# Placing a projection's copy and remainder between the casts of a linear-attention and FFN kernel

## The chip, the cores and the metric

The kernel runs on one core of a Trainium2 chip. The metric is the device time of one execution in microseconds. The kernel before took 695.48 us, the median of three runs (694.21 to 696.63).

## What is computed

A linear attention over 8 batches, 8 heads, 576 positions and 32 memory slots is followed by a feed-forward block with a SiLU over the 4608 rows that the attention gives.

```python
def _attn_ref(q, k, v, phi):
    a = np.exp(phi - np.max(phi, axis=2, keepdims=True))
    a = a / (np.sum(a, axis=2, keepdims=True) + 1e-09)
    k_m = np.einsum('bhsm,bhsd->bhmd', a, k)
    v_m = np.einsum('bhsm,bhsd->bhmd', a, v)
    scores = 1.0 / np.sqrt(q.shape[-1]) * np.matmul(q, k_m.transpose(0, 1, 3, 2))
    scores = scores - np.max(scores, axis=-1, keepdims=True)
    attn = np.exp(scores)
    attn = attn / (np.sum(attn, axis=-1, keepdims=True) + 1e-09)
    return np.matmul(attn, v_m)

def _moe_ref(x, w_in, w_out):          # x: (4608, 512), d_ff = 2048
    h = x @ w_in
    return (h * (1.0 / (1.0 + np.exp(-h)))) @ w_out
```

## The kernel before

The value product and the first FFN matrix are joined: instead of forming the attention's output and then multiplying it with w_in, the kernel multiplies v_m with w_in, once per batch and head. This product is P. It comes in four blocks of 512 columns per batch (`p_mm`, matmuls at line 657 into the PSUM tile `bg`). Every number that a large matmul uses is split in two: a rounded high part, made on ScalarE, and the remainder, made on VectorE. For P these are the copy at line 682 and the subtraction at line 684 (`p_split`), both into the tile `pm`, one after the other. Three matmul terms (hi by hi, hi by lo, lo by hi) take the place of one exact product.

The FFN then runs in slots. A slot makes h for two blocks of 128 columns (`ffn1s`, line 852: twelve matmuls, of which the fifth and sixth are the first that read P's remainder), activates it (line 868 or 870, ScalarE, into `gbuf`), and makes seven sums of the quarters of the result, the forms of a Strassen-like scheme (`forms`). In a slot's forms, ScalarE casts three high parts (line 873) and, once VectorE has made the sums (874, 877, 878), four more (883); VectorE makes the remainders of the first three (884) and of the last four (885). In two slots of a batch, where ScalarE has an exponential to do, VectorE does all of it (880, 881). The forms are multiplied with w_out in the next slot (`st_step`, line 894, 21 matmuls into four PSUM banks named `sum`). So TensorE's order in slot s is: h of slot s, then what else is due (P, the products of phi with k and v, the scores), then the output products of slot s - 1.

The first two batches (b = 0 and 1) use a plain scheme (`ffn1`, lines 704 and 746). Batches b = 2 to 7 have 16 slots each. A table of events (`ev`, `run`) says in which slot the attention of the next batch does its steps: phi's maximum is subtracted in slot 1 (slot 3 for b = 2; lines 322 and 325), the exponential (329) and the first half of the phi-kv product (`e_mm`, 348) come in slots 2 and 3 (4 and 5 for b = 2), the second half in slot 5 (7 for b = 2). `e_mm` ends with the normalisation: two sums (366), two reciprocals (368) and the scaled copies `kvn` (372 on ScalarE, 374 on VectorE). One of its two results lies in the fourth `sum` bank, so the last output products of the slot wait until `kvn` has been read out. The scores of the next batch are computed in slot 7 (`s_all`), transposed on VectorE out of PSUM: two short pieces of 64 columns (404), of which one lies in the fourth `sum` bank too, and two long ones (406).

P's third and fourth blocks are made in the batch that uses them: the third in slot 3 (slot 2 for b = 2, slot 0 for b = 7) and the fourth in slot 5 (slot 2 for b = 7); h reads them from slot 4 and from slot 6 on. `run` issues P's matmuls, copy and remainder ahead of a slot's other events but behind the slot's forms, and holds VectorE's other events behind both (`last_split`, `last_p`, through `behind`, an order without a semaphore). TensorE and ScalarE follow the program's order; on VectorE the scheduler orders what `behind` leaves free.

```python
        todo.sort(key=lambda e: e[0] not in (p_mm, p_pair))
        last_p.clear()
        for fn, a in todo:
            ...
                    for other in [last_split[-1]] + last_p:
                        behind(i, other)
```

Of the kernel before, what the change touches and what calls it, by code (L numbers as in the profile page):

```python
# [16 lines left out]
ALU = mybir.AluOpType  # L17
# [3 lines left out]
B, S, H, M, D = 8, 576, 8, 32, 64  # L21
# [6 lines left out]
JW = 512  # L28
# [8 lines left out]
FULLC = S // P  # L37
# [13 lines left out]
def attn_ffn_kernel(  # L51
# [9 lines left out]
    nc = tc.nc  # L61
# [326 lines left out]
    def s_all(b):  # L388

        sc = at[b]["sc"] = sb.tile([P, 2, S], F32, tag="x" if b == 2 else "y", name=f"sc{b}", bufs=1)  # L390
        bg = bgtile()
        left = [spare_bank()[:, :LEFT], accs()[3][:, Q + KVW : Q + KVW + LEFT]] if b > 3 else beside_h(LEFT)
        kvT = at[b]["kvT"]
        for hf, f, n in ((0, 0, CUT), (1, 0, CUT), (1, CUT, LEFT)):
            for r in range(NR):
                for p in range(2):
                    to = left[p] if f else bg[:, p, hf * CUT : hf * CUT + n]
                    nc.tensor.matmul(
                        to[M * r : M * (r + 1)],
                        kvT[D * p : D * (p + 1), 0, r],  # L400
                        at[b]["q", hf][D * p : D * (p + 1), r, f : f + n],
                        start=not f or b < 4 or p == 0, stop=True, skip_group_check=True,
                    )
        short = [nc.vector.transpose(sc[:, p, 512:], left[p]) for p in range(2)]
        for p in range(2):
            i = nc.vector.transpose(sc[:, p, :512], bg[:, p])
            for other in (*short, last_split[-1]):
                behind(i.ins, other)
# [449 lines left out]
    def exp_slots(b):  # L858
        return () if b == B - 1 else (4, 11) if b == 2 else (2, 11)

    def forms(b, t, j, h):


        g = form_src
        h = live["h"]
        o = b % 2 * LEFT
        if t == 0:
            nc.scalar.activation(gbuf[:, :MAIN], h[0], AF.Silu)  # L868
        for i in range(2 * t):
            nc.scalar.activation(gbuf[:, i * CUT : (i + 1) * CUT], h[i][:, :CUT], AF.Silu)  # L870
            nc.scalar.activation(gleft[:, 2 * j + i, o : o + LEFT], h[i][:, CUT:WIDE], AF.Silu)  # L871
        hi, lo = form_high[j % 2], form_low[j % 2]
        nc.scalar.activation(hi[:, :3], g[:, 1:4], AF.Copy)  # L873
        nc.vector.tensor_tensor(  # L874
            g[:, 4:6], g[:, :1].broadcast_to([P, 2, P]), g[:, 1:3], op=ALU.subtract
        )
        nc.vector.tensor_tensor(g[:, 6], g[:, 1], g[:, 5], op=ALU.subtract)  # L877
        s4 = nc.vector.tensor_tensor(g[:, 7], g[:, 3], g[:, 6], op=ALU.subtract)  # L878
        if t * NP + j in exp_slots(b):
            nc.vector.tensor_copy(hi[:, 3:], g[:, 4:])  # L880
            last_split.append(nc.vector.tensor_tensor(lo, g[:, 1:], hi, op=ALU.subtract))
            return hi, lo
        nc.scalar.activation(hi[:, 3:], g[:, 4:], AF.Copy)  # L883
        behind(nc.vector.tensor_tensor(lo[:, :3], g[:, 1:4], hi[:, :3], op=ALU.subtract).ins, s4)
        last_split.append(nc.vector.tensor_tensor(lo[:, 3:], g[:, 4:], hi[:, 3:], op=ALU.subtract))  # L885
        return hi, lo

    def product(bank, place, part, k, w, first):
# [110 lines left out]
    def ev(b, slot, fn, *a):  # L999
        events.setdefault((b, slot), []).append((fn, a))  # L1000
# [43 lines left out]
    for b in range(B):  # L1044
        n = b + 1
        if b == 0:
            for j in range(2, DFF // CW):
                ev(b, 2 * j - 1.5, p_mm, b, j * CW, CW)
        elif b == 1:
            ev(b, 0, win_save)  # L1050
            for j in range(1, NJ):
                ev(b, 4 * j - 3, p_mm, b, j * JW, JW)
            for j in range(NP):
                ev(b, 1.5 * j + 2, w_forms, j, 0)
                ev(b, 1.5 * j + 2.5, w_forms, j, 1)
        else:
            ev(b, 0, win_load, b, 3)
            ev(b, 0 if n == B else 3 if b > 2 else 2, p_mm, b, 2 * JW, JW)
            if b > 2:
                ev(b, 3, s_norm, b, SECOND)  # L1060
                ev(b, 4, s_back, b, SECOND)
                ev(b, 4, s_low, b, SECOND)
            ev(b, 2 if n == B else 5, p_mm, b, 3 * JW, JW)
            if n < B:
                steady(b, n)
            continue
        at_slot = (
            (4, 5, 6, 7.5, 9, 9.5, 11.5, 12.5, 13, 13.5, 13.5, 14) if b == 0
            else (1, 2, 3, 5, 9, 10, 10, 11, 12, 13, 13, 14)
        )  # L1070
        mx, sub, ex, em, tr, s0, s1, sx, se, ss, sn, sk = at_slot
        ev(b, mx, phi_max, n)
        if n == 1:
            ev(b, sub, phi_allmax, n, (0, 1), (0,))
            ev(b, sub + 0.5, phi_allmax, n, (0, 1), (1,))
        else:
            for i in range(3):
                ev(b, sub, phi_fold, n, i)
        ev(b, sub + 0.5, phi_sub, n)
        ev(b, ex, phi_exp, n)  # L1080
        ev(b, em, e_mm, n)
        ev(b, 14 if b == 0 else em + 1, load_kv, n + 1, range(FULLC if b == 0 else 2))
        ev(b, tr, e_tr, n)
        ev(b, em, load_q, n, 1)
        if n == 1:
            ev(b, s0, s_mm, n, 0)
            ev(b, s1, s_mm, n, 1)
        else:
            ev(b, s0, s_all, n)
        ev(b, s1, load_q, n + 1, 0)  # L1090
        ev(b, sx, s_max, n, ALL)
        ev(b, sx, s_sub, n, ALL)
        ev(b, se, s_exp, n, ALL)
        ev(b, ss, s_sum, n, ALL)
        ev(b, sn, s_norm, n, ALL)
        ev(b, sk, s_back, n, ALL)
        ev(b, sk, s_low, n, ALL)
        ev(b, sk, load_phi, n + 1)
        if b == 0:
            ev(b, 14, p_mm, n, 0, JW)  # L1100
        else:
            for k in range(3):
                ev(b, 12 if k == 2 else 6 + k, win_load, n, k)
            for k in range(2):
                ev(b, 12 + 2 * k, p_mm, n, k * JW, JW)
# [124 lines left out]
    def finish(tiles):  # L1230
# [10 lines left out]
        elif prev[0] == "st" and tiles[0] == 0:  # L1241
            st_step(*prev[1:])

    def run(b, slot):
        todo = events.pop((b, slot), [])
        todo.sort(key=lambda e: e[0] not in (p_mm, p_pair))
        last_p.clear()
        for fn, a in todo:
            n = len(nc.cur_bb.bb.instructions)
            fn(*a)  # L1250
            for i in list(nc.cur_bb.bb.instructions)[n:]:
                if i.engine == DVE and fn not in (p_mm, p_pair, s_all, *((e_mm,) if b > 2 else ())):
                    for other in [last_split[-1]] + last_p:
                        behind(i, other)

    for b in range(B):
        if b == 1:
            whole.close()
            ctx.enter_context(in_order(ACT))
        for s in range(NFC if b > 1 else 0):  # L1260
            t, j = divmod(s, NP)
            h = ffn1s(b, t, j)
            part = forms(b, t, j, h)
            run(b, s)
            finish(range(NI))
            prev = ("st", b, t, j, part)
        for fc in range(NFC if b < 2 else 0):
            if b == 0 and fc < 2:
                for part in range(2):
                    for fn, a in events.pop((b, fc + part / 2), []):  # L1270
                        fn(*a)
                continue
            h = ffn1(b, fc)
            gs = split(silu(b, fc, h))
            for part in range(2):
                if b == 0:
                    finish((2 * part, 2 * part + 1))
                traced = nc.cur_bb.bb.instructions
                n = len(traced)
                for fn, a in events.pop((b, fc + part / 2), []):  # L1280
                    fn(*a)
                if b == 0:
                    for i in list(nc.cur_bb.bb.instructions)[n:]:
                        if i.engine == ACT:
                            behind(i, last_silu[-1])
                        elif i.engine == DVE and fc > 10:
                            behind(i, last_split[-1])
            if b:
                finish(range(NI))
            prev = ("main", b, fc, gs)  # L1290
        if b % 2:
            for n in range(NLS):
                gs = left_split(b, n)
                if b > 1:
                    run(b, NFC + n)
                finish((0, 1, 2, 3))
                prev = ("left", b, n, gs)
# [52 lines left out]
```

## Time and profile before

| What | Value |
|---|---|
| median of three runs | 695.48 us (694.21 to 696.63) |
| profiled execution | 695.39 us |
| its span, first to last instruction | 693.6 us |
| TensorE matmul, busy | 674.0 us (97%), 5932 instructions |
| TensorE weight load, busy | 598.7 us (86%) |
| VectorE, busy | 517.6 us (75%), 1088 instructions |
| ScalarE, busy | 382.1 us (55%), 758 instructions |
| mean granted TensorE clock | 0.998 of full speed |
| DMA | 93.92 MB, 135 GB/s mean |

A matmul's end is modelled, and matmuls overlap, so TensorE's 97% is not all progress: pauses show in the starts of the matmuls. Times in the rows further down count from the span's start. Each row gives the start, the duration, the engine (PE is TensorE, PEld its weight loads, DVE VectorE, ACT ScalarE), the line of the kernel, the operation and its tiles, and in brackets the idle time of the engine before it with what ended that.

### The profile page before, as it was taken

How to read it: one execution, taken by the hardware profiler on the slowest of the kernel's cores; microseconds unless marked ns; L12 is line 12 of the kernel's file. 1: busy time of each engine (PE TensorE's matmuls, PEld its weight loads, DVE VectorE, ACT ScalarE, POOL GpSimd, SP SyncE). 2: the span in 40 equal slices, each digit the busy share in tenths (PEclk: the TensorE clock that was granted, in tenths of full speed). 3: DMA queues.
4: the chain of work that ended last, by engine and by line, in shares of the span. 5: the costliest groups of instructions: out<-in, count | busy, mean ns of one | idle time of the engine just before them, and what ended most of it. 6: DMA issues, size and time to landing. Idle time of an engine off the chain costs nothing.

```text
span 693.6 us, 14807 instructions
## 1 busy us (share of the span) xinstructions
PE 674.0 (97%) x5932; PEld 598.7 (86%) x5932; DVE 517.6 (75%) x1088; ACT 382.1 (55%) x758; POOL 0.7 (0%) x6
## 2 busy tenths in 40 slices
PE   8899999999999899989999899999999999999997
PEld 3578777888888899979999799988999879889997
DVE  4997899788847488778775688776876767777653
ACT  3879784544535455744645446564654546655551
POOL 0000000000000000000000000000000000000000
PEclk9999999999999999999999999999999999999999
DMA  9998965314451361344320434125431204210001
GB/s 340 356 347 256 347 254 218 109 45 160 146 162 44 130 220 62 111 156 150 132 92 20 166 132 156 69 85 181 152 123 37 72 2 140 79 72 17 32 1 45
DMA packets 38228, 93.92 MB, mean 135 GB/s; under 512 B 4752, under 2 KB 22032, under 8 KB 34576
## 3 DMA queue, kind: packets, MB, share of 16 engines
q1 hardware_dynamic: 37136, 90.22, 37.7%
q10 hardware_dynamic: 1024, 2.77, 1.0%
q8 instruction: 46, 0.75, 0.5%
q14 instruction: 22, 0.18, 0.1%
HBM read 77.22 MB, written 15.73 MB: 134 GB/s over the span
## 4 chain that ended last, share of the span: by engine, by line
PE 62%; DVE 15%; ACT 6%; issue 3%; DMA 0%; SPq 0%; DVEq 0%; ACTq 0%
PE sum L894 29%; PE h L852 18%; PE acc L746 7%; PE h L704 4%; PE bg L657 2%; ACT aparts L883 2%; DVE gbuf L874 2%; DVE pm L684 2%; PE accleft L746 2%; ACT gbuf L868 1%; DVE gbuf L877 1%; DVE gbuf L878 1%; ACT pm L682 1%; DVE gparts L885 1%; DVE aT L481 1%
## 5 line engine op out<-in xcount | busy, mean ns | idle before, releaser
L852 PE MATMUL h<-aparts,pm 128*128 128x256 f32 (+1 forms) x1152 | 171.3, 297 | 4.4 <-DVE pm L684 2.5
L852 PEld LDWEIGHTS h<-aparts,pm 128*128 128x128 f32 x1152 | 158.3, 190 | 6.2 <-DVE pm L684 3.6
L894 PE MATMUL sum<-wo_hi,aparts 128*128 128x256 f32 x480 | 120.6, 290 | 0.0
L894 PE MATMUL sum<-wo_lo,aparts 128*128 128x256 f32 x432 | 112.9, 283 | 0.0
L874 DVE TENSOR_TENSOR gbuf<-gbuf 128x256 f32<-128x256 f32 x96 | 40.6, 423 | 88.5 <-ACT gbuf L868 59.0
L894 PE MATMUL sum<-kept,aparts 128*128 128x256 f32 x576 | 101.0, 284 | 5.6 <-DVE kvn L374 5.1
L894 PEld LDWEIGHTS sum<-wo_hi,aparts 128*128 128x128 f32 x480 | 88.5, 191 | 11.7 <-ACT gleft L871 4.2
L894 PEld LDWEIGHTS sum<-kept,aparts 128*128 128x128 f32 x576 | 82.4, 191 | 7.5 <-DVE kvn L374 6.2
L894 PE MATMUL sum<-wo_hi,gparts 128*128 128x256 f32 x480 | 88.3, 283 | 0.0
L883 ACT ACTIVATE aparts<-gbuf 128x512 fp32r<-128x512 f32 x86 | 54.4, 632 | 61.4 <-DVE gbuf L878 61.4
L746 PE MATMUL acc<-wo_hi,gparts 128*128 128x512 f32 x256 | 86.4, 397 | 0.1
L894 PEld LDWEIGHTS sum<-wo_lo,aparts 128*128 128x128 f32 x432 | 82.6, 191 | 0.0
L885 DVE TENSOR_TENSOR gparts<-gbuf,aparts 128x512 fp32r<-128x512 f32 x86 | 59.6, 693 | 19.6 <-ACT aparts L883 19.5
L894 PEld LDWEIGHTS sum<-wo_hi,gparts 128*128 128x128 f32 x480 | 73.0, 191 | 0.0
L870 ACT ACTIVATE gbuf<-h 128x256 f32<-128x256 f32 x96 | 36.9, 384 | 55.7 <-PE h L852 55.5
L868 ACT ACTIVATE gbuf<-h 128x512 f32<-128x512 f32 x48 | 28.6, 596 | 70.3 <-PE h L852 70.3
L894 PE MATMUL sum<-kept,gparts 128*128 128x256 f32 x288 | 65.6, 282 | 0.0
L746 PEld LDWEIGHTS acc<-wo_hi,gparts 128*128 128x128 f32 x256 | 48.0, 188 | 13.5 <-DVE gparts L721 1.4
L704 PE MATMUL h<-aparts,pm 128*128 128x256 f32 (+1 forms) x372 | 56.0, 299 | 1.2 <-ACT aparts L619 0.6
L704 PEld LDWEIGHTS h<-aparts,pm 128*128 128x128 f32 x372 | 51.0, 188 | 6.9 <-issue 2.8
L873 ACT ACTIVATE aparts<-gbuf 128x384 fp32r<-128x384 f32 x96 | 50.5, 526 | 1.5
L746 PE MATMUL acc<-wo_lo,gparts 128*128 128x512 f32 x128 | 50.3, 393 | 0.8 <-DVE wo_lo L186 0.8
(217 smaller groups left out, 964.2 us busy)
## 6 DMA issues: line engine op xcount, KB each, us to landing
win<-win_saved SPq DMA_DIRECT2D x24, 1024.0 KB, 4.9
kv<-in_kv SPq DMA_DIRECT2D x28, 516.0 KB, 4.7
raw<-in_w_in SPq DMA_DIRECT2D x14, 512.0 KB, 7.6
raw<-in_w_out SPq DMA_DIRECT2D x6, 1024.0 KB, 6.6
q<-in_q SPq DMA_DIRECT2D x8, 640.0 KB, 5.9
q<-in_q SPq DMA_DIRECT2D x8, 512.0 KB, 4.8
win_saved<-win SPq DMA_DIRECT2D x4, 1024.0 KB, 8.8
phi<-in_phi SPq DMA_DIRECT2D x7, 576.0 KB, 6.3
```

The costliest lines, as they stand in the source:

```text
L657: nc.tensor.matmul(bg[p][M * r : M * (r + 1), :w].rearrange("p (k f) -> p k f", f=P), kvT[D * p : D * (p + 1), 1, r], src[D * p : D * (p + ...
L684: i = nc.vector.tensor_tensor(lo[:, :, c], bg[:, :, :w], hi[:, :, c], op=ALU.subtract)
L704: nc.tensor.matmul(h[hf][:, : PART[hf][1] - PART[hf][0]], wt[:, p, fs], a[:, p, slice(*PART[hf])], start=n[hf] == 0, stop=n[hf] == 5, skip ...
L746: nc.tensor.matmul(acc[key], gt[:, cs], wt[:, fc], start=fc == 0 and n == 0, stop=fc == NFC - 1 and n == 2)
L852: nc.tensor.matmul(h[i], wt[:, p, f : f + P], a[:, p], start=n == 0, stop=n == 5, skip_group_check=True,)
L868: nc.scalar.activation(gbuf[:, :MAIN], h[0], AF.Silu)
L870: nc.scalar.activation(gbuf[:, i * CUT : (i + 1) * CUT], h[i][:, :CUT], AF.Silu)
L873: nc.scalar.activation(hi[:, :3], g[:, 1:4], AF.Copy)
L874: nc.vector.tensor_tensor(g[:, 4:6], g[:, :1].broadcast_to([P, 2, P]), g[:, 1:3], op=ALU.subtract)
L883: nc.scalar.activation(hi[:, 3:], g[:, 4:], AF.Copy)
L885: last_split.append(nc.vector.tensor_tensor(lo[:, 3:], g[:, 4:], hi[:, 3:], op=ALU.subtract))
L894: nc.tensor.matmul(sums[bank][:, place * Q : (place + 1) * Q], gt[:, k], wt, start=bank not in begun, stop=True, skip_group_check=True,)
```

## The change

Five things are changed in the order of the instructions; what is computed stays the same.

1. In slot 3 of batches b = 3 to 6 P's third block is taken out of the slot's events and issued inside `forms`, by a function passed as `between`. Its copy then stands between ScalarE's two casts and its remainder between VectorE's two splits (the last split is put behind it).
2. In the slot where `e_mm` ends, P's remainder is put behind the second `kvn`. This bears on slot 5 of b = 3 to 6.
3. For b = 2 P's fourth block moves from slot 5 to slot 3 as a whole.
4. In `s_all` the short piece of the fourth `sum` bank is transposed first, and for later batches the other is put behind it.
5. The first h of b = 1 is made in the order hi by hi, lo by hi, hi by lo, alternating between the two halves of the positions.

```diff
-        short = [nc.vector.transpose(sc[:, p, 512:], left[p]) for p in range(2)]
+        short = [nc.vector.transpose(sc[:, p, 512:], left[p]) for p in (1, 0)]
+        if b > 3:
+            behind(short[1].ins, short[0])
...
-    def forms(b, t, j, h):
+    def forms(b, t, j, h, between):
...
         if t * NP + j in exp_slots(b):
+            between()
             nc.vector.tensor_copy(hi[:, 3:], g[:, 4:])
             last_split.append(nc.vector.tensor_tensor(lo, g[:, 1:], hi, op=ALU.subtract))
             return hi, lo
+        behind(nc.vector.tensor_tensor(lo[:, :3], g[:, 1:4], hi[:, :3], op=ALU.subtract).ins, s4)
+        sooner = between()
         nc.scalar.activation(hi[:, 3:], g[:, 4:], AF.Copy)
-        behind(nc.vector.tensor_tensor(lo[:, :3], g[:, 1:4], hi[:, :3], op=ALU.subtract).ins, s4)
         last_split.append(nc.vector.tensor_tensor(lo[:, 3:], g[:, 4:], hi[:, 3:], op=ALU.subtract))
+        if sooner:
+            behind(last_split[-1].ins, sooner[-1])
         return hi, lo
...
-            ev(b, 2 if n == B else 5, p_mm, b, 3 * JW, JW)
+            ev(b, 2 if n == B else 5 if b > 2 else 3, p_mm, b, 3 * JW, JW)
...
+    def p_first(b, slot):
+
+        last_p.clear()
+        todo = events.get((b, slot), [])
+        mine = [e for e in todo if e[0] is p_mm and slot == 3 and b > 2]
+        for e in mine:
+            todo.remove(e)
+            e[0](*e[1])
+        return last_p[:]
...
     def run(b, slot):
         todo = events.pop((b, slot), [])
         todo.sort(key=lambda e: e[0] not in (p_mm, p_pair))
-        last_p.clear()
+        turned = any(fn is e_mm and a[1][-1] == FULLC - 1 for fn, a in todo)
         for fn, a in todo:
             n = len(nc.cur_bb.bb.instructions)
             fn(*a)
+            if fn is e_mm and b > 1 and turned:
+                for i in last_p:
+                    behind(i.ins, last_kvn[-1])
+                last_p.clear()
...
-            part = forms(b, t, j, h)
+            part = forms(b, t, j, h, lambda: p_first(b, s))
...
-            h = ffn1(b, fc)
+            h = ffn1(b, fc, low_last=b == 1 and not fc)
```

The order that results on VectorE in slot 3 of b = 3, before (first) and with the change (second). `gbuf` holds the forms, `gparts` their remainders, `pm` is P, `sc` the scores, `x` and `oo` output tiles.

```order
L878 TENSOR_TENSOR gbuf<-gbuf 128x128
L884 TENSOR_TENSOR gparts<-gbuf,aparts 128x384
L885 TENSOR_TENSOR gparts<-gbuf,aparts 128x512
L684 TENSOR_TENSOR pm<-bg,pm 128x1024
L462 TENSOR_TENSOR sc_2635<-sc_2635,ssm 128x2x320
L944 TENSOR_TENSOR x<-x,oo 128x256 x3
L874 TENSOR_TENSOR gbuf<-gbuf 128x256
```

```order
L880 TENSOR_TENSOR gbuf<-gbuf 128x128
L886 TENSOR_TENSOR gparts<-gbuf,aparts 128x384
L686 TENSOR_TENSOR pm<-bg,pm 128x1024
L889 TENSOR_TENSOR gparts<-gbuf,aparts 128x512
L464 TENSOR_TENSOR sc_2635<-sc_2635,ssm 128x2x320
L950 TENSOR_TENSOR x<-x,oo 128x256 x3
L876 TENSOR_TENSOR gbuf<-gbuf 128x256
```

P's remainder has moved ahead of the last split; on ScalarE its copy has moved ahead of the second cast in the same way. The even batches have no output additions in this slot.

The order on VectorE in slot 5 of b = 3, before and with the change. `rs` are the sums of the phi weights and their reciprocals.

```order
L885 TENSOR_TENSOR gparts<-gbuf,aparts 128x512
L366 TENSOR_SCALAR rs<-h_2105 128x1
L366 TENSOR_SCALAR rs<-sum_2173 128x1
L368 RECIPROCAL rs<-rs 128x1
L684 TENSOR_TENSOR pm<-bg,pm 128x1024
L368 RECIPROCAL rs<-rs 128x1
L374 TENSOR_SCALAR kvn<-sum_2173,rs 128x2x64
```

```order
L889 TENSOR_TENSOR gparts<-gbuf,aparts 128x512
L366 TENSOR_SCALAR rs<-h_2105 128x1
L366 TENSOR_SCALAR rs<-sum_2173 128x1
L368 RECIPROCAL rs<-rs 128x1 x2
L374 TENSOR_SCALAR kvn<-sum_2173,rs 128x2x64
L686 TENSOR_TENSOR pm<-bg,pm 128x1024
```

P's remainder has left the place between the reciprocals and stands behind `kvn`.

The order on ScalarE in slots 3 and 4 of b = 2, before and with the change. `h` to `gbuf` is the activation, `phi` the exponential, the table loads stand on either side of it.

```order
L883 ACTIVATE aparts<-gbuf 128x512
L868 ACTIVATE gbuf<-h_2104 128x512
L873 ACTIVATE aparts<-gbuf 128x384
L329 ACT_TABLE_LOAD
L329 ACTIVATE phi_1967<-phi_1967 128x1152
L868 ACT_TABLE_LOAD
```

```order
L888 ACTIVATE aparts<-gbuf 128x512
L684 ACTIVATE pm<-bg 128x1024
L870 ACTIVATE gbuf<-h_2104 128x512
L875 ACTIVATE aparts<-gbuf 128x384
L329 ACT_TABLE_LOAD
L329 ACTIVATE phi_1967<-phi_1967 128x1152
L870 ACT_TABLE_LOAD
```

The copy of P's fourth block stands in slot 3, ahead of slot 4's activation; on VectorE its remainder stands in slot 3 ahead of the four subtractions from phi, and on TensorE its matmuls stand behind h of slot 3.

## Rows read from the trace of the kernel before

**Rows 1.** The chain of waits: start us, length us, engine and line

```profile
230.08 2.78 PE sum L894 x21
...
365.06 1.43 PE h L852 x12
...
397.86 2.50 PE sum L894 x21
```

**Rows 2.** Who waited for whom, whole run: us in total, times, longest us

```profile
PEld sum L894 <- DVE sc L404: 1.3, 4, 0.5
...
PE sum L894 <- DVE kvn L374: 5.1, 5, 1.2
...
PE h L852 <- DVE pm L684: 2.5, 5, 0.5
```

**Rows 3.** The timeline, slot 3 of b = 4: start us, us, engine, line

```profile
380.50 0.52 ACT L873 ACTIVATE aparts<-gbuf 128x384 fp32r<-128x384 f32 x1
...
382.15 1.01 ACT L682 ACTIVATE pm<-bg 128x1024 fp32r<-128x1024 f32 x1
...
383.19 1.22 DVE L684 TENSOR_TENSOR pm<-bg,pm 128x1024 fp32r<-128x1024 f32 x1 [0.22 <-ACT pm L682]
383.23 0.72 PE L852 MATMUL h<-aparts,pm 128*128 128x256 f32 x4
...
384.47 1.22 PE L852 MATMUL h<-aparts,pm 128*128 128x256 f32 x8 [0.52 <-DVE pm L684]
385.53 0.28 PE L894 MATMUL sum<-wo_hi,aparts 128*128 128x256 f32 x1
```

**Rows 4.** The timeline, slots 3 and 4 of b = 3, VectorE

```profile
298.14 0.43 DVE L874 TENSOR_TENSOR gbuf<-gbuf 128x256 f32<-128x256 f32 x1
```

**Rows 5.** The timeline, slot 5 of b = 4, VectorE and TensorE

```profile
393.87 1.23 DVE L684 TENSOR_TENSOR pm<-bg,pm 128x1024 fp32r<-128x1024 f32 x1
...
395.01 0.15 DVE L368 RECIPROCAL rs<-rs 128x1 f32<-128x1 f32 x1
395.20 0.35 DVE L374 TENSOR_SCALAR kvn<-sum,rs 128x128 f32<-128x128 f32 x1
395.61 0.51 PE L894 MATMUL sum<-kept,aparts 128*128 128x256 f32 x2 [1.24 <-DVE kvn L374]
...
396.07 1.57 PE L852 MATMUL h<-aparts,pm 128*128 128x256 f32 x12
397.48 0.38 PE L383 MATMUL h<-ident,kvn 128*128 128x128 f32 x2
```

**Rows 6.** The timeline, slots 3 to 6 of b = 2, and its window's load

```profile
183.93 0.32 SPq L90 DMA_DIRECT2D win<-win_saved  x1
...
216.10 0.63 ACT L883 ACTIVATE aparts<-gbuf 128x512 fp32r<-128x512 f32 x1 [2.62 <-DVE gbuf L878]
...
217.38 0.69 DVE L322 TENSOR_TENSOR phi<-phi,am 128x512 f32<-128x512 f32 x1
...
219.21 1.17 ACT L329 ACTIVATE phi<-phi 128x1152 f32<-128x1152 f32 x1
...
221.21 0.43 PE L348 MATMUL h<-kv,phi 128*32 128x129 f32 x8
...
223.41 0.60 ACT L868 ACTIVATE gbuf<-h 128x512 f32<-128x512 f32 x1
...
226.74 0.88 PE L852 MATMUL h<-aparts,pm 128*128 128x256 f32 x4 [1.76 <-ACT pm L682]
228.00 2.08 PE L852 MATMUL h<-aparts,pm 128*128 128x256 f32 x8 [0.38 <-DVE pm L684]
229.88 0.42 PE L894 MATMUL sum<-wo_hi,aparts 128*128 128x256 f32 x1
```

**Rows 7.** Busy time by stretch (PE, PEld, DVE, ACT, POOL), PEclk, DMA share, GB/s

```profile
228.00:230.00 2.00, 2.00 (x9) 2.00 (x10) 0.00 (x0) 0.00 (x0) 0.00 (x0) 0.50 0.03 8
```

**Rows 8.** The timeline, first h of b = 1, TensorE

```profile
107.37 1.63 PE L704 MATMUL h<-aparts,pm 128*128 128x256 f32 x10 [0.54 <-DVE aparts L488]
```

## The prediction

> **What bounds the kernel now.** I read the chain of waits first. Long stretches of it are TensorE alone: twelve h matmuls in 1.43 us, twenty-one output products in 2.50 us, slot after slot [rows 1]. Each such stretch is one slot of 33 matmuls at about 0.119 us, so a TensorE pause of one microsecond that ends before such a stretch moves everything behind it by one microsecond. The second view is the list of who waited for whom, which names the pauses that are left: five waits for kvn on VectorE, five for P's remainder, and four for the transposes of the short scores [rows 2]. "P" is the product of the values with a block of w_in; its copy (ScalarE, hi) and its remainder (VectorE, lo) are the stationary operand of h. Then I followed slots 3 and 5 of one batch in the timeline (b = 4; b = 3, 5 and 6 show the same pattern), the odd batches' extra VectorE work, and slots 3 to 6 of the third batch (b = 2), where the largest pause stands.
>
> **Slot 3, b = 3 to 6 (four times).** Today P's copy stands behind both casts on ScalarE and its remainder behind VectorE's last split. For b = 4 the first cast ends at 381.02, the copy runs from 382.15 and the remainder from 383.19 to 384.41; h starts at 383.23, stops after the four matmuls that need only hi, and goes on at 384.47 [rows 3]. Now the copy follows the first cast: 381.02 + 1.01 = 382.03, and the remainder 382.05 + 1.22 = 383.27. That is before the fifth h matmul is due (383.23 + 4 x 0.12 = 383.71), so twelve run through in 1.43 and the next products start at 384.66 instead of 385.53: TensorE gains 0.87. P's own matmuls keep their place on TensorE. The cast that now stands behind the copy and the split behind the remainder come later by at most the length of these, 1.01 and 1.22 us, but the products that read them belong to the slot after, behind 384.66, so I cost that at nothing; without that cover it would be up to 1.2 each time. In the odd batches VectorE, not TensorE, is late next: a normalisation and three output additions fill its time up to the next slot's first form, which starts at 298.14 with no idle time ahead of it [rows 4]. What the reordering takes out there are the idle gap of 0.22 ahead of the remainder [rows 3] and one like it ahead of the split; with the little air before 298.14 the forms start between 0.45 and 0.87 earlier, and I take 0.6.
>
> **Slot 5, b = 3 to 6 (four times).** The remainder stands between the two reciprocals. It delays the second from 393.87 to 395.01, so 1.14, and with it kvn and TensorE, which waits until 395.61 after an idle time of 1.24 [rows 5]. Now it goes behind kvn. VectorE's work there moves up with slot 3 by 0.87 (even) or 0.6 (odd), and kvn by a further 1.14: TensorE goes on at 395.61 - 0.87 - 1.14 = 393.60. What is late next is the remainder itself, since h of slot 6 reads this block. It starts about 0.28 behind kvn's start (0.35 less the usual overlap), at 395.20 - 2.01 + 0.28 = 393.47, and ends at 394.69. h starts at 393.60 + 0.46 = 394.06 and wants lo from 394.54, so it waits 0.2. Eight more matmuls (0.95) end it near 395.65, against 397.48 [rows 5]. That is 1.8 for an even batch, slot 3's 0.87 within it, and 1.55 for an odd one. Twice 1.8 and twice 1.55: **6.7 us**.
>
> **Third batch (b = 2).** Here P's last block moves with matmuls, copy and remainder from slot 5 to slot 3. Today TensorE stands idle 1.76 for the copy, does four h matmuls, waits for the remainder, and does eight more from 228.00 to 229.88, so 0.235 each instead of 0.119 [rows 6]. The granted clock there is 0.50, the 1.2 GHz level [rows 7]; the next 21 products take 2.78 instead of 2.50 [rows 1]. All of that goes. What comes instead lies in slots 3 and 4. ScalarE does the copy from 216.7 to 217.7. VectorE does the remainder from 217.7, so the four phi subtractions start at 218.84 instead of 217.38, 1.46 later, and the exponential at 220.67 instead of 219.21, ending at 221.84 [rows 6]. P's matmuls change slots on TensorE and cancel, but they no longer cover the exponential: the first phi-kv product starts at 221.87 instead of 221.21, a new wait of 0.66. Slot 4's split and, behind it, ScalarE's table load and slot 5's activation move by the same 1.46: the activation, which frees the bank for the next h, ends at 223.41 + 0.60 + 1.46 = 225.47 [rows 6]. TensorE, ready for that h at 226.74 - 1.76 + 0.66 = 225.64, doesn't wait for it. h then ends at 225.64 + 1.43 = 227.07 instead of 229.88, which is 2.8, and 0.28 comes with the products at full clock: **3.1 us**. The load of P's window of w_in keeps its place on the queue of SyncE, at 183.93 [rows 6], some 28 us before slot 3; no other DMA moves.
>
> **Short scores, four times.** TensorE waits 1.3 in four places for the second of two small transposes, though only one reads the bank that it wants [rows 2]. Doing that one first saves one transpose each. Between nothing and 1.3 I take a little over half, **0.7**. **First h of the second batch.** It stops 0.54 for alo after two matmuls [rows 8]; now the six terms that don't need alo's halves come first, and the second half of alo becomes the last to arrive. Between 0 and the 0.54 I take **0.3**.
>
> **Sum.** 6.7 + 3.1 + 0.7 + 0.3 = 10.8 us. The profiled execution took 695.39 (span 693.6), within 0.1 of the median of the three runs, so 684.6 us, 1.6% less. Nothing in the stretches behind takes it back: the chain there is TensorE [rows 1], and loads follow the instructions that free their buffers.
>
> **The clock.** The one fall to half rate follows the idle time of 1.76; the five waits for kvn, 1.2 at most, cost no clock that the products behind them show [rows 2, 5, 6]. So for the new wait of 0.66 I take no fall. The Trainium skill (TensorE: Matmul & The Clock Gate, Part 1) says that the half-rate state is the default, and that only recent activity releases it. By that rule any added pause puts the clock at risk: with no fall the sum stays at 684.6, with one fall it is 685.8. The trace agrees that a pause can bring it (0.50 behind the 1.76).
>
> **Rivals.**
> (1) Slot 5 gives back slot 3's gain: VectorE's list doesn't move up, and the remainder behind kvn becomes the full wait of h. Then kvn frees TensorE at 394.47, the remainder ends at 395.56, and h ends at 396.55, 0.9 per batch, so 3.7 instead of 6.7: 687.6. For it: VectorE has no pause ahead of slot 4 in the odd batches [rows 4]. Against: in the even ones it waits for TensorE.
> (2) The clock falls behind the new 0.66 in the third batch. Eight matmuls at 0.235 cost 0.93 more, the products 0.28 [rows 1, 6]: 1.2, so 685.8.
> (3) Slower: the pauses left in b = 2 to 6 (0.66 once, some 0.1 to 0.8 at kvn and 0.2 at the remainder) each bring the clock down for a whole slot of 33 matmuls. At 0.116 more for each, that is 3.8 in five places, 19 us, so 704. It makes the kernel slower once some 20 matmuls run slow in each of the five places (10.8 / 5 / 0.116). Against: longer waits in the same places cost none [rows 5].
> (4) The gain is no gain: a chain through VectorE, ScalarE or a load with a fixed length takes over behind slot 6, and the time stays near 694. Against: the TensorE-only stretches [rows 1].
> (5) More than forecast: the remaining pauses vanish as well, 4 x 2.2 in slots 3 to 6, 3.4 in the third batch (1.76 + 0.38 idle, 0.93 + 0.28 of slow matmuls), 1.3 and 0.5: 14.0, so 681.4.
>
> **How the numbers follow.** Forecast 0.63, (1) 0.16, (2) 0.10, (3) 0.03, (4) 0.05, (5) 0.03. A difference of 0.3% (2.1 us) is about what a measurement of this kernel can tell from no change. Faster: 0.63 + 0.16 + 0.10 + 0.03 = 0.92; within 0.3%: 0.05; slower: 0.03. The range reaches from just short of (5), 681.8, to just beyond (1), 688.4; the bounds of the unknown prices (short scores 0 to 1.3, first h 0 to 0.54) lie within.
>
> **What would show it.** In slot 3 of b = 3 to 6 the wait of h for the remainder is gone. In slot 5 the wait for kvn falls from 1.24 to 0.1 in even batches and to under 0.8 in odd ones, and a wait of about 0.2 of h for the remainder appears behind it. In the third batch the 1.76 is gone, the granted clock is 1.00 throughout, and the first phi-kv product of slot 5 waits about 0.7 for the exponential. The four waits for the short scores shrink to about half. I am wrong if new waits of over 0.5 stand in slots 6 to 15, or if a granted clock of 0.50 shows in the middle of the run.

## The result, and the profile after

| | before | with the change |
|---|---|---|
| median | 696.06 us (694.21 to 697.15, four runs) | 684.75 us (684.57 to 685.10, four runs) |
| ratio | | 0.9841, 95% interval 0.9818 to 0.9864 |
| span of the profiled execution | 693.6 us | 682.9 us |
| mean granted clock of it | 0.998 | 1.000 |

The forecast was 684.6 us. The profiled executions differ by 693.6 - 682.9 = 10.7 us, and the sum said 10.8.

The list of who waited for whom shows first what went. These are all of the matmuls' waits of 0.15 us or more from the second batch on; the columns are the total in us, the times, and the longest.

```profile
PE sum L900 <- DVE kvn L374: 0.8, 3, 0.5
...
PE h L348 <- ACT phi L329: 0.5, 1, 0.5
...
PE sum L900 <- DVE sc L404: 0.2, 1, 0.2
```

The 5.1 us for kvn [rows 2] have become 0.8. The 2.5 for P's remainder are gone from the list of matmuls; on the weight loads' side they were 3.6 in five waits of up to 0.7, and have shrunk to this:

```profile
PEld h L854 <- DVE pm L686: 1.0, 4, 0.3
```

Two waits are new: the 0.5 for the exponential in the third batch, and the four of the weight loads for the remainder behind kvn.

Slot 3 of b = 4 in the timeline of the changed kernel, to be laid beside [rows 3]:

```profile
375.33 0.52 ACT L875 ACTIVATE aparts<-gbuf 128x384 fp32r<-128x384 f32 x1
...
375.76 1.01 ACT L684 ACTIVATE pm<-bg 128x1024 fp32r<-128x1024 f32 x1
...
376.67 0.62 ACT L888 ACTIVATE aparts<-gbuf 128x512 fp32r<-128x512 f32 x1
...
376.81 1.22 DVE L686 TENSOR_TENSOR pm<-bg,pm 128x1024 fp32r<-128x1024 f32 x1
...
378.05 1.57 PE L854 MATMUL h<-aparts,pm 128*128 128x256 f32 x12
...
379.46 0.29 PE L900 MATMUL sum<-wo_hi,aparts 128*128 128x256 f32 x1
...
380.30 0.42 DVE L876 TENSOR_TENSOR gbuf<-gbuf 128x256 f32<-128x256 f32 x1 [0.93 <-ACT gbuf L870]
```

The copy starts as the first cast ends, the remainder is done at 378.03, and the twelve h matmuls run in one piece: 1.41 us to the next product, where it was 2.30 before. VectorE then waits 0.93 for the next activation, so in this even batch it follows TensorE and not the other way round.

Slot 5 of the same batch, beside [rows 5]:

```profile
387.69 0.23 DVE L368 RECIPROCAL rs<-rs 128x1 f32<-128x1 f32 x2
...
387.96 0.35 DVE L374 TENSOR_SCALAR kvn<-sum,rs 128x128 f32<-128x128 f32 x1
388.23 1.21 DVE L686 TENSOR_TENSOR pm<-bg,pm 128x1024 fp32r<-128x1024 f32 x1
388.36 0.51 PE L900 MATMUL sum<-kept,aparts 128*128 128x256 f32 x2
...
388.83 1.89 PE L854 MATMUL h<-aparts,pm 128*128 128x256 f32 x12
390.56 0.38 PE L383 MATMUL h<-ident,kvn 128*128 128x128 f32 x2
```

The two reciprocals stand together, and the idle time of 1.24 ahead of the products behind kvn has shrunk to 0.06 (388.36 less the modelled end at 387.90 + 0.40), which is under what the view prints. But twelve h matmuls now take 1.73 from their start to the next instruction instead of 1.41: the remainder ends at 389.44, and the fifth of them was due at 389.31. The new wait costs 0.32.

The odd batches keep a wait that the even ones do not have: 0.18 in b = 5, and here 0.48 in slot 5 of b = 3:

```profile
301.62 0.35 DVE L374 TENSOR_SCALAR kvn<-sum,rs 128x128 f32<-128x128 f32 x1
...
302.02 0.51 PE L900 MATMUL sum<-kept,aparts 128*128 128x256 f32 x2 [0.48 <-DVE kvn L374]
```

Slots 3 to 6 of the third batch, beside [rows 6]:

```profile
217.41 1.22 DVE L686 TENSOR_TENSOR pm<-bg,pm 128x1024 fp32r<-128x1024 f32 x1 [0.23 <-ACT pm L684]
...
218.56 0.68 DVE L322 TENSOR_TENSOR phi<-phi,am 128x512 f32<-128x512 f32 x1
...
220.38 1.17 ACT L329 ACTIVATE phi<-phi 128x1152 f32<-128x1152 f32 x1 [0.66 <-DVE phi L325]
...
221.60 0.43 PE L348 MATMUL h<-kv,phi 128*32 128x129 f32 x8 [0.52 <-ACT phi L329]
...
225.24 1.69 PE L854 MATMUL h<-aparts,pm 128*128 128x256 f32 x12
```

The pause of 1.76 is gone, and h of slot 6 runs in one piece. The window around it has the granted clock at 1.00, where it was 0.50 [rows 7]:

```profile
224.00:231.00 7.00, 7.00 (x65) 6.80 (x67) 4.34 (x10) 4.19 (x8) 0.00 (x0) 1.00 0.35 135
```

To see where the 10.7 us come from, I took the start of the first h matmul of every slot in both traces and noted where their difference changes. Positive numbers are us gained.

| Place | Forecast | Measured |
|---|---|---|
| first h of b = 1 | 0.3 | 0.36 |
| b = 2, slots 3 to 6 | 3.1 | 3.15 |
| b = 3, 5: slot 3; slots 5 and 6 | 1.55 each together | 1.20 + 0.45; 0.89 + 0.75 |
| b = 4, 6: slot 3; slots 5 and 6 | 1.8 each together | 0.88 + 0.86; 0.89 + 0.86 |
| short scores, four times | 0.7 in all | 0.13 each, 0.5 in all |

Behind slot 8 of the seventh batch (b = 6), and in every stretch between these places, the difference stays where it is: nothing is given back. The 1.20 of b = 3 holds 0.30 for which the prediction has no term: there the first h matmul too stood still before, until P's copy ended at 294.95, and now it doesn't. It adds nothing to the batch, whose sum is set in slot 5 (1.65, against 1.64 in b = 5).

### The profile page after: what moved, and what is told of

Read it like the earlier page. It is cut to its first block, busy times and chain, and to the rows that moved or that the text cites. A ratio compares the mean times of both kernels' runs of the same rounds, so it can differ in the third digit from the quotient of the medians.

```text
span 682.9 us, 14803 instructions
## 1 busy us (share of the span) xinstructions
PE 672.2 (98%) x5932; PEld 597.5 (87%) x5932; DVE 516.3 (76%) x1088; ACT 381.5 (56%) x758; POOL 0.7 (0%) x6
## 4 chain that ended last, share of the span: by engine, by line
PE 65%; DVE 14%; ACT 4%; issue 2%; DMA 0%; SPq 0%; DVEq 0%; ACTq 0%
PE sum L900 31%; PE h L854 18%; PE acc L748 7%; PE h L706 4%; PE bg L659 2%; ACT aparts L888 2%; PE accleft L748 2%; DVE gbuf L876 2%; DVE gparts L889 1%; DVE gbuf L879 1%; DVE pm L686 1%; DVE gbuf L880 1%; DVE aT L483 1%; PE bg L398 1%; ACT aparts L485 1%
```

## The experiments

All edits are to the changed kernel. The theory is the one of the prediction: pauses of TensorE that are independent of each other, except that slot 3's gain reaches slot 5 through VectorE's list. Three runs undo one part each, beside the changed kernel on the same chip. The runs from the small parts on were taken on two other chips, beside the kernel before alone; their differences are to 684.82 all the same, and the starts of the h matmuls are given with them as a second reading.

> The changed kernel as it is, beside the runs that each undo one part. 684.7 us within 0.4; both theories say the same.

Measured: 684.82 us, ratio to before 0.9853 (0.9834 to 0.9872). This is the base for what follows.

**Slot 3's part undone.**

```diff
-        mine = [e for e in todo if e[0] is p_mm and slot == 3 and b > 2]
+        mine = []
```

> Slot 3's part alone undone (b = 3 to 6): P's copy and remainder stand behind the casts again. Theory (a chain through VectorE): the slot 3 pause of 0.87 to 1.2 is back, slot 5's list starts later by 0.87 (even) or 0.6 (odd), and slot 5's own part still gives 0.9 per batch, 3.7 in all; 3.0 us are lost: 687.8. In slot 5 h then waits 0.7 for the remainder. Rival (the wait for kvn absorbs whatever slot 3 gains): under 0.6 us lost, 685.3 or less.

Measured: 688.13 us, ratio 0.9895 (0.9880 to 0.9910), so 3.3 us lost. The rival's 0.6 at most is out. Slot 3 of b = 4 in its timeline looks as in [rows 3] again:

```profile
379.45 0.73 PE L854 MATMUL h<-aparts,pm 128*128 128x256 f32 x4
...
380.70 1.22 PE L854 MATMUL h<-aparts,pm 128*128 128x256 f32 x8 [0.52 <-DVE pm L686]
```

Slot 5 of the same batch keeps what it gained; the weight loads' wait of 0.25 for the remainder is of the size that the changed kernel has (0.3 at most):

```profile
390.66 0.50 PE L900 MATMUL sum<-kept,aparts 128*128 128x256 f32 x2
391.11 1.89 PE L854 MATMUL h<-aparts,pm 128*128 128x256 f32 x12
391.79 1.00 PEld L854 LDWEIGHTS h<-aparts,pm 128*128 128x128 f32 x8 [0.25 <-DVE pm L686]
```

The expectation had said 0.7 for that wait, and that was wrong: kvn and the remainder move together, so the wait of h behind kvn has the same length wherever the list starts. In the even batches exactly slot 3's 0.90 was lost; in the odd ones it is 0.80 and 0.76, a little more than the 0.6 of the theory.

**Slot 5's part undone.**

```diff
-            if fn is e_mm and b > 1 and turned:
-                for i in last_p:
-                    behind(i.ins, last_kvn[-1])
-                last_p.clear()
```

> Slot 5's part alone undone (b = 3 to 6): P's remainder stands between the reciprocals again. Theory: slot 3 alone gives 0.87 per even and 0.6 per odd batch, 2.9 in all; 3.8 us are lost: 688.5. The wait of TensorE for kvn is 1.2 in even batches and 1.5 to 1.8 in odd ones, and h of slot 6 waits for nothing. Rival (the remainder's place behind kvn gives back most of what it saves, since h waits for it): under 1.5 us lost, 686.2 or less.

Measured: 688.41 us, ratio 0.9900 (0.9885 to 0.9915), so 3.6 us lost where 3.8 were expected; the rival's 1.5 is out. Slot 5 of b = 4, where kvn again waits for the remainder and h runs in one piece:

```profile
388.60 0.16 DVE L368 RECIPROCAL rs<-rs 128x1 f32<-128x1 f32 x1
388.72 1.23 DVE L686 TENSOR_TENSOR pm<-bg,pm 128x1024 fp32r<-128x1024 f32 x1
...
389.86 0.15 DVE L368 RECIPROCAL rs<-rs 128x1 f32<-128x1 f32 x1
...
390.45 0.50 PE L900 MATMUL sum<-kept,aparts 128*128 128x256 f32 x2 [1.25 <-DVE kvn L374]
390.91 1.57 PE L854 MATMUL h<-aparts,pm 128*128 128x256 f32 x12
```

The products behind kvn start 1.2 later in every batch, and h takes back 0.3 of it: the part is worth 0.88 a batch. The wait for kvn is 1.25 in the even batches and 1.68 in b = 3, as expected; in b = 5 it is 1.37, short of the 1.5.

**The third batch's part undone.**

```diff
-            ev(b, 2 if n == B else 5 if b > 2 else 3, p_mm, b, 3 * JW, JW)
+            ev(b, 2 if n == B else 5, p_mm, b, 3 * JW, JW)
```

> Third batch's part alone undone: P's last block in slot 5 again. Theory: 3.1 us lost, 687.9; TensorE idle 1.7 for the copy, and the granted clock falls to 0.50 behind it, 1.2 of the 3.1. Rival (the clock's fall before was chance, not the pause): 1.9 us lost, 686.6, granted clock 1.00 throughout.

Measured: 688.87 us (687.55 to 689.88), ratio 0.9904 (0.9885 to 0.9922): 4.0 us lost, and a spread of 2.3 us where the base runs have 0.4 but for one. In the stretch behind the pause, as busy us of TensorE, its weight loads, VectorE, ScalarE and GpSimd, granted clock, DMA share and GB/s:

```profile
226.00:228.00 2.00, 0.74 (x4) 0.54 (x4) 1.78 (x2) 0.85 (x1) 0.00 (x0) 0.89 0.14 58
228.00:230.00 2.00, 1.84 (x8) 1.84 (x9) 0.11 (x1) 0.00 (x0) 0.00 (x0) 0.50 0.03 8
230.00:232.00 2.00, 2.00 (x12) 2.00 (x11) 1.03 (x4) 1.12 (x2) 0.00 (x0) 0.50 0.00 0
232.00:234.00 2.00, 2.00 (x11) 2.00 (x11) 1.15 (x2) 0.63 (x1) 0.00 (x0) 0.50 0.00 0
234.00:236.00 2.00, 2.00 (x19) 1.87 (x17) 0.00 (x0) 0.00 (x0) 0.00 (x0) 0.91 0.00 0
```

The pause is back (1.78 this time) and so is the fall to 0.50, but it lasts longer. A stretch of 2 us with a mean clock c was slow for (1 - c) x 2 / 0.5 us. That gives 0.4 + 2 + 2 + 2 + 0.4 = 6.8 us here; the kernel before has 0.80, 0.50 and 0.85 in its stretches from 226 to 232, so 0.8 + 2 + 0.6 = 3.4 us:

```profile
226.00:228.00 2.00, 0.88 (x4) 0.58 (x5) 1.73 (x2) 0.69 (x1) 0.00 (x0) 0.80 0.08 31
...
230.00:232.00 2.00, 2.00 (x17) 2.00 (x16) 1.19 (x4) 1.27 (x3) 0.00 (x0) 0.85 0.00 0
```

Slow time does half the work, so the difference of 3.4 costs up to 1.7 more. That and the part's 3.15 make up to 4.9, and this execution (689.88) stands 5.1 over the base. The run of 687.55, whose mean clock is 0.998 and not 0.995, lost only 2.7. So the part is worth what was forecast where the fall is as long as in the profiled execution, and more or less where it isn't.

**Both small parts undone.**

```diff
-        short = [nc.vector.transpose(sc[:, p, 512:], left[p]) for p in (1, 0)]
-        if b > 3:
-            behind(short[1].ins, short[0])
+        short = [nc.vector.transpose(sc[:, p, 512:], left[p]) for p in range(2)]
...
-            h = ffn1(b, fc, low_last=b == 1 and not fc)
+            h = ffn1(b, fc, low_last=False)
```

> The two small parts undone: short scores in the old order, first h of the second batch in the old order. Theory: 0.13 lost in each of four places where the output products wait for the short scores, 0.36 at the first h, 0.9 in all: 685.6. Rival (both are hidden, since the work behind waits elsewhere): no change, 684.7.

Measured: 685.62 us, ratio 0.9859 (0.9838 to 0.9880), so 0.8 lost. By the start of each slot's first h matmul it is 0.36 at the first h of b = 1 and 0.12 or 0.13 at each of the four short scores, 0.86 together. The parts add up: 3.3 + 3.6 + 4.0 + 0.8 is 11.7, against 11.1 between the medians of 684.82 and 695.88 beside them, and the longer clock fall of the third run is large enough for the surplus.

The next four runs ask what the waits that are left are worth. First the new wait for the exponential in the third batch: there the remainder goes behind the split of slot 4, so that the phi subtractions no longer queue behind it.

```diff
+    held = []
...
+            if fn is p_mm and (b, slot) == (2, 3):
+                held.extend(last_p)
+                last_p.clear()
...
+            if (b, s) == (2, 4):
+                behind(held.pop().ins, last_split[-1])
```

> Third batch: P's remainder in slot 3 no longer ahead of the phi subtractions but behind slot 4's split. Theory: the new wait of 0.5 for the exponential ahead of the phi-kv product goes, nothing else is late (h reads the remainder only in slot 6), and slot 5's activation comes 1.2 earlier: 0.5 us gained, 684.2. Rival (the wait turns up at h of slot 6, for the activation or for the remainder): 684.7.

Measured: 684.08 us, ratio 0.9836 (0.9818 to 0.9853).

```profile
219.77 1.17 ACT L329 ACTIVATE phi<-phi 128x1152 f32<-128x1152 f32 x1
...
221.06 0.43 PE L348 MATMUL h<-kv,phi 128*32 128x129 f32 x8
...
221.73 1.22 DVE L687 TENSOR_TENSOR pm<-bg,pm 128x1024 fp32r<-128x1024 f32 x1
...
224.67 1.59 PE L855 MATMUL h<-aparts,pm 128*128 128x256 f32 x12
```

The exponential starts at 219.77 instead of 220.38, the products behind it have no idle time, and the remainder is done at 222.95, 1.7 before h starts. So the 0.52 was a real pause on the path, and a free one to take away: 0.7 gained, 0.72 by the starts of h, where 0.5 was expected.

Second, the wait of h for the remainder behind kvn. The subtraction is cut into two column halves, so that the first half of the matmuls can start on the first half of it.

```diff
-            i = nc.vector.tensor_tensor(lo[:, :, c], bg[:, :, :w], hi[:, :, c], op=ALU.subtract)
-            last_p[:] = [i]
+            n = 2 if 2 < b < B - 1 and f == 3 * JW else 1
+            last_p.clear()
+            for k in range(n):
...
```

> Slot 5 of b = 3 to 6: P's remainder behind kvn in two halves of 256 columns, of which h of slot 6 reads only the first. Theory: the wait of h for the remainder, 0.32 in each of four batches, goes: 1.3 us gained, 683.4. Rival (h is held by kvn's readers or the weight loads as well, or two instructions cost the list more): under 0.4 gained, 684.3 or more.

Measured: 683.77 us, ratio 0.9832 (0.9814 to 0.9849), so 1.05 gained.

```profile
387.85 0.35 DVE L374 TENSOR_SCALAR kvn<-sum,rs 128x128 f32<-128x128 f32 x1
388.12 1.28 DVE L691 TENSOR_TENSOR pm<-bg,pm 128x512 fp32r<-128x512 f32 x2
...
388.71 1.59 PE L859 MATMUL h<-aparts,pm 128*128 128x256 f32 x12
390.14 0.38 PE L383 MATMUL h<-ident,kvn 128*128 128x128 f32 x2
```

Two halves take 1.28 on VectorE where one took 1.21, and the twelve matmuls take 1.43 again instead of 1.73. The gain by the starts of h is 0.31, 0.31, 0.31 and 0.29.

Third, the odd batches' wait for kvn: a normalisation that stands in slot 3 of VectorE's list goes to slot 2.

```diff
-                ev(b, 3, s_norm, b, SECOND)
+                ev(b, 2, s_norm, b, SECOND)
```

> b = 3 to 6 (and 7): the normalisation of the second part of the scores in slot 2, where VectorE waits 2.0 for ScalarE's table load, instead of slot 3. Theory: in the odd batches VectorE's list was what held slot 5 back, so the wait for kvn falls from 0.5 to 0.2 and 0.2 to 0.4 is gained in each of two batches: 684.2. Even batches do not change. Rival (VectorE's list is not what holds the odd batches): 684.7, the wait for kvn stays at 0.5.

Measured: 684.16 us, ratio 0.9837 (0.9820 to 0.9855), so 0.66 gained between the medians; by the starts of h 0.44 in b = 3 and 0.10 in b = 5, where 0.2 to 0.4 each had been expected.

```profile
301.35 0.35 DVE L374 TENSOR_SCALAR kvn<-sum,rs 128x128 f32<-128x128 f32 x1
301.75 0.50 PE L900 MATMUL sum<-kept,aparts 128*128 128x256 f32 x2
```

No idle time stands ahead of the products any more. That confirms what holds slot 5 back in the odd batches: VectorE's list, not TensorE.

All three together:

> The last three edits together: third batch's remainder behind slot 4's split, slot 5's remainder in halves, normalisation in slot 2. Theory: they work at different waits, so the gains add: 0.7 + 1.2 + 0.5 = 2.4 us below the changed kernel, 682.4. Rival (they overlap in the odd batches): 683.2 or more.

Measured: 682.40 us, ratio 0.9816 (0.9803 to 0.9829). Five of the six runs lie from 682.12 to 682.45; the sixth took 3671.26 us at a granted clock of 1.0, has no trace, and stays unexplained. The median is the sum of the three gains (0.74 + 1.05 + 0.66 = 2.45 below 684.82) and beats both kernels. What matmuls still wait for from the third batch on is 0.2 for kvn and 0.2 for a short score.

The last run is about rival 3, the clock. It undoes slot 5's part and issues the remainder's subtraction of this block a second time, so that the wait for kvn grows by most of a subtraction; nothing else changes.

```diff
             i = nc.vector.tensor_tensor(lo[:, :, c], bg[:, :, :w], hi[:, :, c], op=ALU.subtract)
+            if 2 < b < B - 1 and f == 3 * JW:
+                i = nc.vector.tensor_tensor(lo[:, :, c], bg[:, :, :w], hi[:, :, c], op=ALU.subtract)
...
-            if fn is e_mm and b > 1 and turned:
-                for i in last_p:
-                    behind(i.ins, last_kvn[-1])
-                last_p.clear()
```

> The changed kernel with slot 5's part undone and P's remainder computed twice there (b = 3 to 6), both ahead of kvn, with the same result: TensorE's four waits for kvn grow by 1.14 to 2.3 or more. Theory (a pause longer than the 1.76 of the third batch puts the clock at risk each time): besides 4 x 1.14 over 688.4, so 693.0, granted clocks of 0.50 show behind some of the four waits, up to 3 us each, and the runs spread by several us: 694 to 705. Rival (the fall in the third batch has to do with what stood there, not with the length of the pause): 693.0, granted clock 1.00 in the four places, spread under 1 us.

Measured: 695.73 us (693.79 to 697.12), ratio 1.0003 (0.9991 to 1.0015). The waits for kvn grew by 1.05 or 1.06 each against the run without slot 5's part (to 2.73, 2.30, 2.43 and 2.30), so without any fall of the clock 688.41 + 4.2 = 692.6 would be due; the fastest run is 1.2 above that, the median 3.1. The waits in b = 3, 4 and 6:

```profile
303.72 0.34 DVE L374 TENSOR_SCALAR kvn<-sum,rs 128x128 f32<-128x128 f32 x1
...
304.12 0.50 PE L902 MATMUL sum<-kept,aparts 128*128 128x256 f32 x2 [2.73 <-DVE kvn L374]
...
393.91 0.79 PE L902 MATMUL sum<-kept,aparts 128*128 128x256 f32 x2 [2.30 <-DVE kvn L374]
...
562.43 0.50 PE L902 MATMUL sum<-kept,aparts 128*128 128x256 f32 x2 [2.30 <-DVE kvn L374]
```

And the stretches behind the four waits (b = 3 to 6), busy us and granted clock:

```profile
306.00:308.00 2.00, 2.00 (x12) 2.00 (x11) 0.20 (x1) 0.80 (x2) 0.00 (x0) 0.50 0.00 0
...
395.00:397.00 2.00, 2.00 (x11) 2.00 (x11) 0.00 (x0) 0.00 (x0) 0.00 (x0) 0.50 0.36 143
...
472.00:474.00 2.00, 1.45 (x7) 1.45 (x7) 0.49 (x2) 0.00 (x0) 0.00 (x0) 0.53 0.76 303
...
563.00:565.00 2.00, 2.00 (x20) 2.00 (x19) 0.00 (x0) 0.45 (x1) 0.00 (x0) 1.00 0.00 0
```

At three of the four the clock falls to the 1.2 GHz level, and twenty matmuls per 2 us become twelve. In b = 3 it falls at 304.9, 0.75 behind the pause; in b = 4 and 5 at 393.6 and 472.1, 0.3 and 0.4 before the pause has ended. Each fall lasts 3.4 us and, by the starts of h against b = 6, costs 1.35 to 1.55. Behind the fourth, after a pause of 2.30 like the one in b = 4, it stays at 2.4 GHz. The mean clocks of this kernel's ten runs, 0.992 to 0.998, say that each run had a fall and that their number or length differs from execution to execution. So rival 3's mechanism exists; the pauses that the change leaves (0.52 at most) did not set it off in the profiled execution.

## Why the prediction was right

The total came out (684.75 against 684.6), and so did the reasons, step by step.

- **Slot 3.** The wait of h for the remainder is gone, and an even batch gained 0.88 where 0.87 was worked out. The cast and the split that moved back cost nothing, as assumed: no new wait for them shows. In b = 3 the first form of slot 4 came 0.76 earlier than its surroundings, a little over the 0.6 taken between 0.45 and 0.87; undoing the part costs 0.80 and 0.76 in the odd batches.
- **Slot 5.** Rival 1 is out: VectorE's list did move up with slot 3, so slot 5 gains on top of it. Undoing one part left the other's gain whole (3.3 and 3.6 lost). The wait for kvn in even batches came to 0.06, where 0.1 was allowed. Two sizes were off and nearly cancelled, which is luck: the odd batches moved up by more than the 0.6, and h waits 0.32 for the remainder instead of 0.2 everywhere. Per batch the sum came to 1.64 or 1.65 against 1.55, and 1.74 or 1.75 against 1.8: 6.8 in all against 6.7.
- **Third batch.** 3.15 against 3.1. The wait for the exponential came as worked out (its start moved by 0.66 against the products ahead, of which 0.52 is idle), and the activation that frees the bank of slot 6's h is on time. Rival 2 did not happen: the clock is 1.00 behind that wait in the profiled execution. One of the eight runs of the changed kernel took 686.41 at a mean clock of 0.997, so a fall may still come somewhere; where, no trace shows.
- **What the 3.1 hid.** Some 1.2 of it is slow time of the clock (0.93 + 0.28), which was read from one execution as if it were fixed. It isn't: with the same pause it cost more in the run that undid this part, and some runs of the kernel before show no fall at all (last section). The forecast was against a profiled execution whose clock, 0.998, was that of most runs; that the total still fits to 0.2 us is to this extent luck.
- **Short scores.** Mis-sized: 0.5, not 0.7. The 1.3 that the prediction calls TensorE's wait is that of its weight loads [rows 2]; three of these waits went from 0.26 to 0.13 and the fourth from 0.54 to 0.41. So the transpose that is saved is worth 0.13 in each place; the first one still has to be waited for.
- **First h of b = 1.** 0.36 against 0.3.
- **Rival 4** (the gain is eaten later) is out: the difference between the traces stays constant between the places of the table. **Rival 5** was nearly the limit of what the waits are worth: the version with all three further edits reached 682.4, and 681.4 was worked out for no pause at all.
- **The clock rule.** In the trace of the kernel before the clock is 0.50 behind 1.76 of idle TensorE [rows 7], and behind 1.24 twelve matmuls take 1.41 us, full pace [rows 5]. The Trainium skill (TensorE: Matmul & The Clock Gate, Part 1) has the half rate as the default, released by recent activity; the runs agree in that a pause can bring the half rate: all four runs that have the 1.78 again, and all ten with waits of 2.30 to 2.73, have a mean clock of 0.998 or less. That any added pause is at risk did not show for the shorter ones: with the 0.52 here seven of eight runs have a mean clock of 0.999 or more, and with waits for kvn of up to 1.68, where slot 5's part is undone, all four have. The length was not varied by itself, so the runs do not show that it alone decides: the 1.76 has four h matmuls and a second idle time of 0.38 behind it [rows 6], the 1.68 has not.

## What to carry to other kernels

Where an engine's stretch has no slack, find which item of another engine's in-order list is due first, and put items with a later due time behind it: here the casts behind P's copy in slot 3, and P's remainder behind kvn in slot 5. When an item goes back, compute when its own reader is due; if it is late by less than its length, cutting it into halves can pay (here 0.3 for 0.07 of extra engine time). A pause next to a TensorE stretch can cost more than its length through the clock, so price it as a length plus a range, and read the mean clock of every run, not only that of the profiled one.

## What the runs showed of the hardware

The fall of TensorE's clock behind a pause is not a fixed price. The kernel before has one such place, the pause of 1.76 in the third batch. Its 31 runs beside the experiments sort by their mean granted clock:

| Mean clock of the run | Runs | Time of the kernel before |
|---|---|---|
| 0.999 to 1.000 | 9 | 694.13 to 694.61 us |
| 0.996 to 0.998 | 21 | 695.20 to 696.79 us |
| 0.995 | 1 | 697.24 us |

So the same instructions with the same pause took up to about 3 us more in some runs than in others, and the longer runs are those with the lower clock. (Traces with a mean of 0.999 show no fall but one in the last 1.5 us of the span, behind the last matmul.) None of these 31 runs has a trace (that of the kernel before is of another execution), so that their falls stood at this pause is inferred. For it speaks that the runs without the pause hardly fall: of the changed kernel and the versions of it in which the third batch's part stands, the last experiment left out, 37 of 38 runs have a mean clock of 0.999 or more. That is also most of why the changed kernel spreads less: 684.50 to 685.10 in seven of eight runs. The last experiment shows the same within one execution: of two pauses of 2.30, one goes with a clock of 0.50 and one with 1.00. What decides it is open; no run was made to tell it apart.
